# A fused attention and mixture-of-experts kernel: weight tiles moved to the last turns and behind the last stores, late tiles cut into paced pieces

## The chip, the cores and the metric

One core of a Trainium2 chip. The metric is device microseconds of one execution; before the change three runs gave 456.1, 458.65 and 459.66 us, a median of 458.65 us.

## The reference: what is computed

```python
# attention: q, k, v of (8 batches, 8 heads, 576 rows, 64)
scores = 0.125 * q @ k.T ; masked to blocks of 64: block_i >= block_j
attn = exp(scores - max) / (sum + 1e-9) ; x = attn @ v      # x: (4608 tokens, 512)
# experts: 8, capacity 80
expert = argmax(x @ w_gate) ; gate = softmax value of it
for e in range(8):
    tok = the up to 80 tokens of expert e with the highest gate
    out[tok] = gate[tok] * (relu(x[tok] @ w1[e]) @ w2[e])    # w1[e]: 512x1024, w2[e]: 1024x512
# all other rows of out are zero; everything is float32
```

## The kernel before, in words

**Attention.** The work is 32 head pairs (8 batches of 4). A loop of turns `i` runs the list TURN: in turn `i` pair `i` makes its scores and its softmax, pair `i-1` its transposes and values, pair `i+1` is prepared (`prep`: a transpose of q or k on VectorE, for q also a scaling on GpSimd), pair `i+3` is loaded (eight loads of 72 KB in runs of 128 bytes, from SyncE) and the v of pair `i+2`. Three buffers `ld` hold the loads, so that SyncE may run up to three pairs ahead. `max_4` (L459 in the trace) comes once in every turn. After the four pairs of a batch its attention output (unnormalised, in the tile Y) is stored to a DRAM scratch `xs` by four transfers of 288 KB from SyncE (`store`, L289), with the reciprocal row sums beside it (L286, L287), and the gate's logits are made. While this runs, GpSimd writes 18 blocks of 512 KB of zeros to the output.

**Between.** After the last pair come, in a chain on VectorE, TensorE, ScalarE and GpSimd, the last batch's logits and gate, the choice of tokens by expert, and the token numbers `gi`. Then GpSimd issues eight gathers (`xg`, L745) of 80 rows of `xs` each, one for each expert. The first one waits for `gi` and for all stores to `xs`.

**Experts.** For each expert: the rows are normalised and transposed, 128 small matmuls give the hidden layer (`ps`, L845), 128 more the output (`av`, L845), which is transposed back, scaled and scattered. Each matmul has its own weight load. The 16 weight tiles of 2 MB (w1[0], w1[1], w2[0], w1[2], w2[1], ...) have nine buffers: three are there during attention (pool `wp`), six lie where attention's buffers were (`fwa`, `fwc`, `fwb`). The three early tiles are loaded by six transfers of 1 MB from GpSimd in turns 6, 10, 14, 18, 22 and 26 (`early`, L590). All 13 others come from SyncE (`weights`, L242), 2 MB each: six wait for the second gather's data, the other seven for a buffer, that is for the matmuls that read the tile nine places earlier.

**What sets the order.** Attention and the last batch's gate stand in the order of the program (a manual schedule). What follows is placed by a planner with a timeline of its own, queue by queue. Each queue runs its instructions in its order; an instruction that waits holds up those behind it.

Of the kernel before, what the change touches and what calls it, by code (L numbers as in the profile page):

```python
# [18 lines left out]
P = 128  # L19
BLK = 64  # L20
NT = 5
FW0, FWA, FWC, FWB = 3, 3, 1, 2
WARM = [8, 14, 5, 2, 12]
NCAND = 12
CHUNK = 80
# [53 lines left out]
def tile_attn_moe(ctx, tc, q, k, v, w_gate, w1, w2, capacity, out, xs=None, dbg=None):  # L79
    nc = tc.nc  # L80
    B, H, S, D = q.shape
# [20 lines left out]
    if xs is None:  # L102
        xs = dram.tile([NTOK, XW], F32, name="xs")
# [18 lines left out]
    for i in range(4):  # L122
        r = slice(32 * i, 32 * i + 32)
# [19 lines left out]
    rows = 2 * P  # L143
# [25 lines left out]
    before = const.tile([P, P], F32, name="before")  # L169
    after = const.tile([P, P], F32, name="after")  # L170
# [51 lines left out]

    wlist = [(w1, 0)] + [x for e in range(E) for x in ((w1, e + 1), (w2, e))][0:-2] + [(w2, E - 1)]
    wt_ = {}

    def early():
        for w_, view in ((wt_[src is w2, e], src[e].rearrange("(a p) f -> p a f", p=P)) for src, e in wlist[0:FW0]):
            na = w_.shape[1]
            for a in range(0, na, na // 2):
                yield w_[:, a:a + na // 2], view[:, a:a + na // 2]  # L230

    def weights(n, after=None):

        nonlocal nw
        for _ in range(n):
            src, e = wlist[nw]
            w_ = wpools[nw % len(wpools)].tile([P, KP * F], F32, name="w")
            nw += 1
            wt_[src is w2, e] = w_ = w_.rearrange("p (a f) -> p a f", f=src.shape[2])
            if nw <= FW0:  # L240
                continue
            load = nc.sync.dma_start(w_, src[e].rearrange("(a p) f -> p a f", p=P))  # L242
            if after is not None:
                tc.add_manual_dep(load.ins, after.name, mybir.DependencyInfo(
                    mybir.DependencyClass.Sync, mybir.DependencyReason.DATA))

# [14 lines left out]
    class Batch:  # L263
# [17 lines left out]

            nc.vector.transpose(self.Y[:, :, pr], self.xT[:, pr])

        def store(self):
            rows = xs[self.b * S:(self.b + 1) * S]
            nc.sync.dma_start(rows[0:512, DM:DM + H].rearrange("(t p) h -> p t h", p=P), self.rs[:, 0:NT - 1])  # L286
            nc.sync.dma_start(rows[512:S, DM:DM + H], self.rs[0:BLK, NT - 1])  # L287
            for i in range(4):
                self.stored = nc.sync.dma_start(rows[:, i * P:(i + 1) * P].rearrange("(j r) c -> r j c", r=32),  # L289
                                                self.Y[32 * i:32 * i + 32].rearrange("r j a c -> r j (a c)"))  # L290

# [262 lines left out]
    n = B * NP  # L554
    pairs = [Pair(i) for i in range(n)]
# [15 lines left out]
    with tc.manual_schedule():  # L571
        warm(WARM[0], ps_m.tile([P, 512], F32, name="pm"))
        constants()
        constants2()
        for i in range(-3, n + 2):
            if i == -1:
                nc.sync.dma_start(ci, capacity.bitcast(U32).partition_broadcast(P))
                for h in range(2):
                    nc.sync.dma_start(wgd[h * D:(h + 1) * D, :, h * E:(h + 1) * E], wg_v[h])

            if i >= 4 and (i % 2 or i % 8 == 4) and i < n:
                clear(cleared)
                cleared += 1
            if i == 5:
                capacities()
            if i == 4:
                weights(FW0)
                halves = early()
            if i in range(6, 6 + 8 * FW0, 4):
                nc.gpsimd.dma_start(*next(halves))  # L590
            for d, what, *args in TURN:
                if what == "step":
                    step()
                elif 0 <= i + d < n and not (what == "flip" and i + d >= n - NP):
                    getattr(pairs[i + d], what)(*args)
            if n - NP <= i - 1 < n:
                pairs[i - 1].flip()
            if i >= 2 and (i - 2) % NP == NP - 1 and i - 2 < n - 1:
                bt = batches[(i - 2) // NP]
                todo += [(bt.recip,), (bt.store,), (bt.logits, 0), (bt.logits, 1), (bt.logits2, 0), (bt.logits2, 1), (bt.gate,),  # L600
                         (bt.turn, nc.gpsimd)] + [(bt.turn2,)]
        while cleared < nz:
            clear(cleared)
            cleared += 1
        while todo:
            step()
        bt = batches[B - 1]
        bt.recip()
        bt.store()
        bt.logits(0)  # L610
        bt.logits(1)
        bt.logits2(0, (3, NT))
        bt.logits2(1, (3, NT))
        bt.gate()
        bt.turn(nc.vector, 2)
        bt.turn2()
# [16 lines left out]
    tw = dict(reuse_waits="tile")  # L633
    fwa = late.enter_context(tc.tile_pool(name="fwa", bufs=FWA, **right, **tw))
    wpools += [fwa] * FWA
    sel2 = late.enter_context(tc.tile_pool(name="sel2", bufs=1, **right, **tw))


# [41 lines left out]
    HOLD = 1  # L680
# [59 lines left out]
    xg, fetches = [], []  # L740
# [82 lines left out]
    fwc = late.enter_context(tc.tile_pool(name="fwc", bufs=FWC, **right, **tw))  # L823
    fwb = late.enter_context(tc.tile_pool(name="fwb", bufs=FWB, **tw))
    wpools += [fwc] * FWC + [fwb] * FWB
    weights(FWA + FWC + FWB, fetches[HOLD])

    def divide(dst, src):

# [270 lines left out]
```

## Time and profile before

| | |
|---|---|
| runs | 456.1, 458.65, 459.66 us |
| the profiled execution | 455.05 us, its span 453.2 us |
| TensorE busy | 409.2 us (90% of the span) |
| VectorE, ScalarE, GpSimd busy | 283.5, 271.4, 67.7 us |
| mean granted clock of TensorE | 0.975 |
| data moved | 84.41 MB, 64.91 of them on SyncE's hardware queue, 18.16 on GpSimd's software queue |
| packets under 512 bytes | 196925 of 230219 |

How to read it: the profiled execution lies 3.6 us below the median of the three runs and 1.05 us below the fastest of them. Busy shares are means over stages with different limits. The span has three: attention up to about 324 us from its start, the choice of tokens up to about 343 us, the experts up to 445 us. A row of a timeline begins with its start and its length in us; "SPq" and "POOLq" are the queues of SyncE and GpSimd, whose DMA rows show the issuing alone, and the data lands later.

### The profile page before, as it was taken

To read this page: it belongs to the slowest core of one execution; us is meant where nothing else is said; L and a number is where in the kernel's file an instruction comes from. 1 tells how busy PE (TensorE), PEld (TensorE's weight loads), DVE (VectorE), ACT (ScalarE), POOL (GpSimd) and SP (SyncE) were. 2 spreads that over 40 slices of the span, in tenths; PEclk is the share of its full clock that TensorE was granted. 3 is DMA by queue.
4 is the path that set the end of the run, shared out by engine and by line. 5 is a ranking of instruction groups with operands and counts; after the bars stand their busy time and mean duration, and the time that the engine had idled before them with its cause. 6 is when DMAs were issued, how large, how long until landed. Compare 5 with 4: busy or idle time off the path is not lost.

```text
span 453.2 us, 15524 instructions
## 1 busy us (share of the span) xinstructions
PE 409.2 (90%) x6427; PEld 290.4 (64%) x6427; DVE 283.5 (63%) x564; ACT 271.4 (60%) x863; POOL 67.7 (15%) x136
## 2 busy tenths in 40 slices
PE   5899999999999999999999899799868888887991
PEld 3566666666666666666666566465647777777981
DVE  5667887888798798788878679585763212111111
ACT  1688888788798788878878697578321201010100
POOL 5001120111021012111102111010037000000010
PEclk9699999999999999999999999989997999999997
DMA  9678898798889789889779787855047999999110
GB/s 130 103 128 168 172 199 173 140 227 173 186 164 226 133 192 200 194 165 223 163 125 195 174 189 138 174 131 106 15 93 233 352 397 400 394 398 381 45 32 19
DMA packets 230219, 84.41 MB, mean 186 GB/s; under 512 B 196925, under 2 KB 215357, under 8 KB 230144
## 3 DMA queue, kind: packets, MB, share of 16 engines
q1 hardware_dynamic: 222528, 64.91, 64.0%
q0 software_dynamic: 5248, 18.16, 11.8%
q8 instruction: 52, 0.85, 0.8%
q10 hardware_dynamic: 2368, 0.30, 0.5%
q14 instruction: 23, 0.19, 0.1%
HBM read 63.21 MB, written 20.33 MB: 184 GB/s over the span
## 4 chain that ended last, share of the span: by engine, by line
PE 73%; DVE 7%; DMA 6%; SPq 4%; issue 4%; ACT 4%; POOL 0%; POOLq 0%; ACTq 0%; DVEq 0%
PE pm L529 19%; PE sc L434 13%; PE pm L499 9%; PE ps L845 9%; PE av L845 8%; PE sc L450 7%; DMA ld<-in_q_dram 4%; SPq L401 2%; DVE negm L459 2%; PE pm L299 2%; ACT P L468 2%; SPq L289 2%; PE pm L482 1%; ACT P L463 1%; DVE negm L455 1%
## 5 line engine op out<-in xcount | busy, mean ns | idle before, releaser
L463 ACT ACTIVATE P<-sc,negm 128x128 f32<-128x128 f32 (+3 forms) x256 | 133.1, 530 | 23.2 <-DVE negm L455 21.4
L455 DVE TENSOR_REDUCE negm<-sc 128x2 f32<-128x1024 f32 (+3 forms) x128 | 100.1, 809 | 36.6 <-PE sc L441 36.5
L434 PE MATMUL sc<-T,T 64*128 64x128 f32 (+3 forms) x512 | 94.1, 466 | 9.0 <-ACT P L463 7.5
L499 PEld LDWEIGHTS pm<-ident,P 64*128 64x128 f32 x1536 | 57.2, 141 | 33.5 <-ACT P L468 10.0
L499 PE MATMUL pm<-ident,P 64*128 64x64 f32 x1536 | 69.6, 231 | 1.9 <-DVE prod L317 0.4
L434 PEld LDWEIGHTS sc<-T,T 64*128 64x128 f32 x512 | 42.1, 189 | 30.0 <-ACT P L463 10.7
L529 PE MATMUL pm<-PT,vn 128*64 128x128 f32 (+1 forms) x512 | 60.7, 379 | 0.0
L419 POOL TENSOR_SCALAR T<-T 128x576 f32<-128x576 f32 x32 | 21.3, 665 | 235.0 <-DVE T L416 191.2
L416 DVE STREAM_TRANSPOSE T<-ld 128x576 f32<-128x576 f32 x64 | 48.7, 761 | 10.2 <-DMA ld<-in_q_dram 10.1
L463 ACT ACTIVATION_READ_ACCUMULATOR P<-sc,negm 128x1 f32 x256 | 52.8, 206 | 0.0
L529 PE MATMUL pm<-PF,vn 128*64 128x64 f32 (+1 forms) x768 | 48.6, 249 | 0.9 <-ACT PF L539 0.9
L529 PEld LDWEIGHTS pm<-PT,vn 128*64 128x64 f32 x512 | 33.5, 137 | 22.9 <-issue 22.9
L845 PE MATMUL ps<-xsT,w 128*64 128x80 f32 x1024 | 40.7, 239 | 6.8 <-issue 6.8
L539 ACT COPY PF<-pm 128x512 f32<-128x512 f32 x64 | 34.4, 589 | 16.4 <-PE pm L499 16.4
L541 DVE COPY PT<-pm 128x512 f32<-128x512 f32 x64 | 43.5, 680 | 0.5 <-PE pm L499 0.5
L845 PEld LDWEIGHTS ps<-xsT,w 128*64 128x64 f32 x1024 | 38.3, 141 | 8.5 <-issue 8.0
L845 PE MATMUL av<-hT,w 128*64 128x80 f32 x1024 | 38.4, 234 | 5.5 <-issue 5.5
L845 PEld LDWEIGHTS av<-hT,w 128*64 128x64 f32 x1024 | 36.5, 137 | 7.5 <-issue 7.5
L450 PE MATMUL sc<-T,T 64*64 64x288 f32 x256 | 39.4, 427 | 0.6 <-ACT P L463 0.6
L539 ACT COPY PT<-pm 128x512 f32<-128x512 f32 x64 | 37.8, 590 | 0.0
L865 ACT ACTIVATE hT<-ps 128x320 f32<-128x320 f32 x16 | 7.0, 437 | 51.1 <-PE ps L845 51.1
L529 PEld LDWEIGHTS pm<-PF,vn 128*64 128x64 f32 x768 | 32.3, 138 | 7.5 <-ACT PF L539 1.1
(166 smaller groups left out, 390.1 us busy)
## 6 DMA issues: line engine op xcount, KB each, us to landing
w<-in_moe_w_dram SPq DMA_DIRECT2D x13, 2048.0 KB, 21.3
ld<-in_q_dram SPq DMA_DIRECT2D x128, 72.0 KB, 3.5
out_dram<-zero POOLq DMA_DIRECT2D x18, 512.0 KB, 4.0
xs<-Y SPq DMA_DIRECT2D x32, 288.0 KB, 5.0
ld<-in_k_dram SPq DMA_DIRECT2D x124, 72.0 KB, 2.9
vn<-in_v_dram SPq DMA_DIRECT2D x64, 128.0 KB, 3.2
w<-in_moe_w_dram POOLq DMA_DIRECT2D x6, 1024.0 KB, 6.5
vt<-in_v_dram SPq DMA_DIRECT2D x32, 32.0 KB, 3.0
```

What stands on the lines that cost most here:

```text
L289: self.stored = nc.sync.dma_start(rows[:, i * P:(i + 1) * P].rearrange("(j r) c -> r j c", r=32), self.Y[32 * i:32 * i + 32].rearrange("r ...
L416: nc.vector.transpose(t, self.nat[x].rearrange("p g d -> p (g d)"))
L419: nc.gpsimd.tensor_scalar(t, t, scalar1=SCALE, scalar2=1.0, op0=ALU.mult, op1=ALU.mult)
L434: nc.tensor.matmul(s[:, h, c:c + P * (u + 1)], lhsT=self.T[0][r, P * u:P * (u + 1)], rhs=self.T[1][r, 0:P * (u + 1)], start=(x == 0), stop ...
L450: nc.tensor.matmul(s[r, c, 0:288], lhsT=self.T[0][r, 512:S], rhs=self.T[1][r, 288 * c:288 * (c + 1)], start=True, stop=True)
L455: nc.vector.tensor_reduce(self.negm[:, u], self.s[g][:, :, c:c + P * (u + 1)], axis=AX.X, op=ALU.max, negate=True)
L463: nc.scalar.activation(Pt[self.i % 2][u][:, h], self.s[g][:, h, c:c + P * (u + 1)], AF.Exp, bias=self.negm[:, u, h:h + 1], scale=1.0, accu ...
L499: nc.tensor.transpose(pt[c][:, n_ * BLK:(n_ + 1) * BLK], from_[r, P * j:P * (j + 1)], ident[r, r])
L529: nc.tensor.matmul(to, lhsT=lhs, rhs=rhs, start=(n_ == 0), stop=(n_ == len(steps) - 1))
L539: nc.scalar.copy(*self.out.pop((what, x)))
L541: nc.vector.tensor_copy(*self.out.pop((what, x)))
L845: yield nc.tensor.matmul(dst(b)[64 * c:64 * (c + 1)], lhsT=w_[:, a, col:col + 64], rhs=x_[:, a], start=(a == 0), stop=(a == n - 1))
```

## The change

- Four tiles are early (FW0 4 instead of 3; FWB 1 instead of 2, so still nine buffers). Each is one transfer of 2 MB from GpSimd, one in each of the turns 28 to 31, in place of the six of 1 MB in turns 6 to 26.
- The last batch's x is stored pair by pair (`store_pair`): four transfers of 72 KB in runs of 128 bytes for each pair, 16 in all, in place of four transfers of 288 KB in runs of 512 bytes after the last pair.
- Two more tiles (w2[1], w1[3]) are asked for right after attention's buffers are closed, without a wait for a gather, as whole transfers of 2 MB.
- The other ten tiles are loaded in four pieces of 512 KB each. A piece waits for the landing of the third piece before it. The first three of these tiles still wait for the second gather, the other seven for a buffer.

```diff
--- before.py
+++ after.py
@@ -19,7 +19,8 @@
 P = 128
 BLK = 64
 NT = 5
-FW0, FWA, FWC, FWB = 3, 3, 1, 2
+FW0, FWA, FWC, FWB = 4, 3, 1, 1
+PARTS, UNDERWAY = 4, 3
 WARM = [8, 14, 5, 2, 12]
 NCAND = 12
 CHUNK = 80
@@ -222,14 +223,9 @@
 
     wlist = [(w1, 0)] + [x for e in range(E) for x in ((w1, e + 1), (w2, e))][0:-2] + [(w2, E - 1)]
     wt_ = {}
-
-    def early():
-        for w_, view in ((wt_[src is w2, e], src[e].rearrange("(a p) f -> p a f", p=P)) for src, e in wlist[0:FW0]):
-            na = w_.shape[1]
-            for a in range(0, na, na // 2):
-                yield w_[:, a:a + na // 2], view[:, a:a + na // 2]
-
-    def weights(n, after=None):
+    parts_ = []
+
+    def weights(n, after=None, parts=PARTS):
 
         nonlocal nw
         for _ in range(n):
@@ -238,11 +234,16 @@
             nw += 1
             wt_[src is w2, e] = w_ = w_.rearrange("p (a f) -> p a f", f=src.shape[2])
             if nw <= FW0:
+                nc.gpsimd.dma_start(w_, src[e].rearrange("(a p) f -> p a f", p=P))
                 continue
-            load = nc.sync.dma_start(w_, src[e].rearrange("(a p) f -> p a f", p=P))
-            if after is not None:
-                tc.add_manual_dep(load.ins, after.name, mybir.DependencyInfo(
-                    mybir.DependencyClass.Sync, mybir.DependencyReason.DATA))
+            view = src[e].rearrange("(a p) f -> p a f", p=P)
+            na = w_.shape[1]
+            for a in range(0, na, na // parts):
+                load = nc.sync.dma_start(w_[:, a:a + na // parts], view[:, a:a + na // parts]).ins
+                for before in ((after,) if after is not None else ()) + tuple(parts_[-UNDERWAY:][:1] if len(parts_) >= UNDERWAY else ()):
+                    tc.add_manual_dep(load, before.name, mybir.DependencyInfo(
+                        mybir.DependencyClass.Sync, mybir.DependencyReason.DATA))
+                parts_.append(load)
 
 
 
@@ -281,11 +282,17 @@
 
             nc.vector.transpose(self.Y[:, :, pr], self.xT[:, pr])
 
-        def store(self):
+        def store_pair(self, pr):
+            rows = xs[self.b * S:(self.b + 1) * S]
+            for i in range(4):
+                nc.sync.dma_start(rows[:, i * P + 32 * pr:i * P + 32 * pr + 32].rearrange("(j r) c -> r j c", r=32),
+                                  self.Y[32 * i:32 * i + 32, :, pr])
+
+        def store(self, whole=True):
             rows = xs[self.b * S:(self.b + 1) * S]
             nc.sync.dma_start(rows[0:512, DM:DM + H].rearrange("(t p) h -> p t h", p=P), self.rs[:, 0:NT - 1])
             nc.sync.dma_start(rows[512:S, DM:DM + H], self.rs[0:BLK, NT - 1])
-            for i in range(4):
+            for i in range(4 if whole else 0):
                 self.stored = nc.sync.dma_start(rows[:, i * P:(i + 1) * P].rearrange("(j r) c -> r j c", r=32),
                                                 self.Y[32 * i:32 * i + 32].rearrange("r j a c -> r j (a c)"))
 
@@ -583,11 +590,8 @@
                 cleared += 1
             if i == 5:
                 capacities()
-            if i == 4:
-                weights(FW0)
-                halves = early()
-            if i in range(6, 6 + 8 * FW0, 4):
-                nc.gpsimd.dma_start(*next(halves))
+            if n - 4 <= i < n - 4 + FW0:
+                weights(1)
             for d, what, *args in TURN:
                 if what == "step":
                     step()
@@ -595,6 +599,7 @@
                     getattr(pairs[i + d], what)(*args)
             if n - NP <= i - 1 < n:
                 pairs[i - 1].flip()
+                pairs[i - 1].bt.store_pair(pairs[i - 1].pr)
             if i >= 2 and (i - 2) % NP == NP - 1 and i - 2 < n - 1:
                 bt = batches[(i - 2) // NP]
                 todo += [(bt.recip,), (bt.store,), (bt.logits, 0), (bt.logits, 1), (bt.logits2, 0), (bt.logits2, 1), (bt.gate,),
@@ -606,7 +611,7 @@
             step()
         bt = batches[B - 1]
         bt.recip()
-        bt.store()
+        bt.store(False)
         bt.logits(0)
         bt.logits(1)
         bt.logits2(0, (3, NT))
@@ -633,6 +638,7 @@
     tw = dict(reuse_waits="tile")
     fwa = late.enter_context(tc.tile_pool(name="fwa", bufs=FWA, **right, **tw))
     wpools += [fwa] * FWA
+    weights(2, parts=1)
     sel2 = late.enter_context(tc.tile_pool(name="sel2", bufs=1, **right, **tw))
 
 
@@ -823,7 +829,7 @@
     fwc = late.enter_context(tc.tile_pool(name="fwc", bufs=FWC, **right, **tw))
     fwb = late.enter_context(tc.tile_pool(name="fwb", bufs=FWB, **tw))
     wpools += [fwc] * FWC + [fwb] * FWB
-    weights(FWA + FWC + FWB, fetches[HOLD])
+    weights(FWA - 2 + FWC + FWB, fetches[HOLD])
 
     def divide(dst, src):
 
```

Where the instructions now stand. First SyncE's queue at the end of attention (`ld`, `vn` and `vt` are loads of q, k and v, `xs<-Y` stores of x, `xs<-rs` of the row sums, `w` weight tiles). Before:

```order
L409 DMA vn<-in_v_dram 128x4x64 x2
L411 DMA vt_136<-in_v_dram 64x2x64
L286 DMA xs<-rs 128x4x8
L287 DMA xs<-rs 64x8
L289 DMA xs<-Y 32x18x128 x4
L286 DMA xs<-rs 128x4x8
L287 DMA xs<-rs 64x8
L289 DMA xs<-Y 32x18x128 x4
L242 DMA w<-in_moe_w_dram 128x4x1024
L242 DMA w<-in_moe_w_dram 128x8x512
```

Of the change:

```order
L418 DMA vt_136<-in_v_dram 64x2x64
L288 DMA xs<-Y 32x18x32 x4
L293 DMA xs<-rs 128x4x8
L294 DMA xs<-rs 64x8
L296 DMA xs<-Y 32x18x128 x4
L288 DMA xs<-Y 32x18x32 x8
L242 DMA w<-in_moe_w_dram 128x8x512
L242 DMA w<-in_moe_w_dram 128x4x1024
L288 DMA xs<-Y 32x18x32 x4
L293 DMA xs<-rs 128x4x8
L294 DMA xs<-rs 64x8
L242 DMA w<-in_moe_w_dram 128x2x512 x4
```

Before, the stores of the last two batches stood ahead of all weights. Now two tiles of 2 MB stand behind the third pair's stores and ahead of the last pair's four stores and the row sums.

Second, GpSimd's queue in the last turns (`T` is the scaling of q, once in a turn; `zero` the clearing of the output). Before:

```order
L419 TENSOR_SCALAR T_4236<-T_4236 128x576
L590 DMA w<-in_moe_w_dram 128x4x512
L419 TENSOR_SCALAR T_4384<-T_4384 128x576
L150 DMA out_dram<-zero 128x1024
L419 TENSOR_SCALAR T_4549<-T_4549 128x576
L150 DMA out_dram<-zero 128x1024
L270 MEMSET sums 64x8
L419 TENSOR_SCALAR T_4720<-T_4720 128x576
L356 TENSOR_TENSOR sp<-Gm,sameE 128x320
L150 DMA out_dram<-zero 128x1024
L419 TENSOR_SCALAR T_4884<-T_4884 128x576
L419 TENSOR_SCALAR T_5022<-T_5022 128x576
```

Of the change:

```order
L151 DMA out_dram<-zero 128x1024
L237 DMA w<-in_moe_w_dram 128x4x1024
L271 MEMSET sums 64x8
L426 TENSOR_SCALAR T_4713<-T_4713 128x576
L363 TENSOR_TENSOR sp<-Gm,sameE 128x320
L151 DMA out_dram<-zero 128x1024
L237 DMA w<-in_moe_w_dram 128x4x1024
L426 TENSOR_SCALAR T_4879<-T_4879 128x576
L237 DMA w<-in_moe_w_dram 128x8x512
L426 TENSOR_SCALAR T_5023<-T_5023 128x576
L151 DMA out_dram<-zero 128x1024
L237 DMA w<-in_moe_w_dram 128x4x1024
```

The scalings in the first list are those of pairs 26 to 31, in the second those of pairs 29 to 31. The last 1 MB stood between the scalings of pairs 26 and 27; now 2 MB stand ahead of the scaling of pair 29, 2 MB ahead of that of pair 30, 2 MB ahead of that of pair 31, and 2 MB behind it.

## Rows read from the trace of the kernel before

**Rows 1.** Page: busy us by engine; DMA share by slices; queue of instructions.

```profile
PE 409.2 (90%) x6427; PEld 290.4 (64%) x6427; DVE 283.5 (63%) x564; ACT 271.4 (60%) x863; POOL 67.7 (15%) x136
...
DMA  9678898798889789889779787855047999999110
...
q8 instruction: 52, 0.85, 0.8%
```

**Rows 2.** Timeline of VectorE, L459: start, length; one in each turn.

```profile
205.76 0.72 DVE L459 TENSOR_REDUCE negm<-sc 128x1 f32<-128x576 f32 x1
...
233.82 0.76 DVE L459 TENSOR_REDUCE negm<-sc 128x1 f32<-128x576 f32 x1 [0.41 <-PE sc L450]
243.64 0.72 DVE L459 TENSOR_REDUCE negm<-sc 128x1 f32<-128x576 f32 x1
...
284.13 0.72 DVE L459 TENSOR_REDUCE negm<-sc 128x1 f32<-128x576 f32 x1
297.93 0.76 DVE L459 TENSOR_REDUCE negm<-sc 128x1 f32<-128x576 f32 x1 [1.40 <-PE sc L450]
...
317.00 0.76 DVE L459 TENSOR_REDUCE negm<-sc 128x1 f32<-128x576 f32 x1 [1.09 <-PE sc L450]
```

**Rows 3.** Chain of waits, 200 to 290 us: start, length, what.

```profile
285.87 3.76 DMA ld<-in_q_dram
```

**Rows 4.** Timeline of SyncE's queue: start and length of the issuing.

```profile
78.07 4.23 SPq L401 DMA_DIRECT2D ld<-in_q_dram  x4
...
111.87 0.54 SPq L286 DMA_DIRECT2D xs<-rs  x1
...
232.94 0.54 SPq L286 DMA_DIRECT2D xs<-rs  x1
...
238.17 4.40 SPq L401 DMA_DIRECT2D ld<-in_q_dram  x4
```

**Rows 5.** Timeline of VectorE: transposes of q of pairs 10 and 26.

```profile
93.47 0.76 DVE L416 STREAM_TRANSPOSE T<-ld 128x576 f32<-128x576 f32 x1
...
246.11 0.78 DVE L416 STREAM_TRANSPOSE T<-ld 128x576 f32<-128x576 f32 x1 [1.02 <-DMA ld<-in_q_dram]
```

**Rows 6.** Groups by line, TensorE, 344 to 445 us: busy, mean ns, idle before.

```profile
L845 PE MATMUL ps<-xsT,w 128*64 128x80 f32 x1024 | 40.7, 239 | 6.8 <-issue 6.8
L845 PE MATMUL av<-hT,w 128*64 128x80 f32 x1024 | 38.4, 234 | 5.5 <-issue 5.5
```

**Rows 7.** Timeline of TensorE: the first and the last of the idle pieces.

```profile
355.54 2.02 PE L845 MATMUL ps<-xsT,w 128*64 128x80 f32 x52 [0.98 <-issue]
...
418.50 3.95 PE L845 MATMUL ps<-xsT,w 128*64 128x80 f32 x107 [1.38 <-issue]
```

**Rows 8.** Stretches: length, busy time by engine, clock, DMA share, GB/s.

```profile
354.00:418.00 64.00, 52.17 (x1292) 48.39 (x1287) 9.81 (x30) 6.67 (x16) 3.75 (x4) 1.00 1.04 392
418.00:444.00 26.00, 24.31 (x635) 23.18 (x635) 3.71 (x6) 1.75 (x4) 2.74 (x3) 1.00 0.15 49
```

**Rows 9.** Timeline of GpSimd: two clearings of the output, start and length.

```profile
267.19 0.58 POOL L150 DMA_DIRECT2D out_dram<-zero  x1
...
282.43 0.59 POOL L150 DMA_DIRECT2D out_dram<-zero  x1
```

**Rows 10.** Timeline of VectorE: Y of pair 30 is ready after this.

```profile
319.50 0.77 DVE L282 STREAM_TRANSPOSE Y<-xT 128x576 f32<-128x576 f32 x1
```

**Rows 11.** Chain of waits, 290 to 453 us: the first gather's issue begins.

```profile
338.17 0.03 POOLq L745
```

**Rows 12.** DMA view, 317 to 340 us, in 40 slices of 0.575 us.

```profile
GB/s 0 0 0 0 28 0 0 0 0 0 0 0 0 0 0 0 18 13 45 177 177 179 173 175 181 282 198 181 182 117 16 0 0 0 0 0 0 0 0 0
```

**Rows 13.** Page, DMA issues: count, KB each, median us to landing.

```profile
w<-in_moe_w_dram SPq DMA_DIRECT2D x13, 2048.0 KB, 21.3
...
xs<-rs SPq DMA_DIRECT2D x8, 2.0 KB, 1.7
```

**Rows 14.** Timeline of SyncE's queue: the first late weight tiles.

```profile
343.90 6.87 SPq L242 DMA_DIRECT2D w<-in_moe_w_dram  x3
```

## The prediction, made before the changed kernel ran

> **What bounds the kernel now.** I read the page's slices first, then the chain of waits, the timelines of VectorE and SyncE through attention, and the stretches of the expert stage. TensorE is busy for most of the span, so what counts is where it stands still. There are two such places, and the DMA engines are behind both [rows 1].
>
> Attention first. L459 comes once in a turn, so it is a clock. From 205.76 to 243.64 us a batch of four turns takes 37.88 us [rows 2]; this is TensorE's own pace. From 243.64 to 317.00 there are seven turns in 73.36 us; at the pace before they would take 37.88 + 28.06 (205.76 to 233.82) = 65.94. So 7.4 us are lost at the end of attention, most in one turn (284.13 to 297.93, 13.8 us), and there the chain goes through a load of q [rows 3]. The reason is a slow drift. SyncE issues without a break, and its stores of the row sums come every (232.94 - 111.87)/3 = 40.4 us [rows 4], 2.5 us slower than the batches. The lead melts: q of pair 10 was all issued at 82.3 and used at 93.5, a lead of 11.2 us; q of pair 26 at 242.6 and 246.1, a lead of 3.5 us, and that is where VectorE first waits for data [rows 4, 5]. Under about 3.5 us there is a stall.
>
> Experts next. L845 is busy for 79 us and has 12.3 us of idle time, put down to nothing that the profile shows [rows 6]. It is in eleven pieces of about 1.1 us, one every 6.3 us, from 355 to 418 us [rows 7]. From 354 to 418 the DMA engines are full (share 1.04, 392 GB/s) and TensorE is idle for 11.8 us of 64; from 418 on, at a share of 0.15, the pieces are gone [rows 8]. The weights are never waited for. One piece comes for each 128 matmuls with their 128 weight loads, and TensorE's instructions come by DMA in 52 packets of 16 KB for 12854 instructions, about 247 each [rows 1]. I read the pieces as blocks of instructions that arrive late while the DMA engines are full. So this stage is bound by TensorE, and fewer bytes help only by making the full stretch shorter or its queue shallower.
>
> **The change, part by part.**
>
> *Six early loads leave turns 6 to 26.* That is 1 MB a batch, at 392 GB/s [rows 8] 2.7 us of all DMA engines. 40.4 - 2.7 = 37.7 us a batch, just under the batch's 37.9: the drift stops and the lead stays near 11 us. The 7.4 us of stall go. Bounds: 0 (the drift has another cause) and 7.4.
>
> *Four loads of 2 MB come in turns 28 to 31.* The first two stand on GpSimd's queue just behind the clearings at 267 and 282 us [rows 9], the others later. Each takes 2.1 MB/392 GB/s = 5.35 us. The first delays the loads of pair 30, the second those of pair 31; no q or k comes later. 11.2 - 5.35 = 5.9 us of lead is enough for pair 30; 11.2 - 10.7 = 0.5 us is 3 us too little for pair 31 if nothing is caught up between. I take 1 us, bounds 0 and 3. The issuing itself (0.6 us for 512 KB [rows 9], so at most 2.4) costs nothing: GpSimd is busy for 15% of the span [rows 1], and without that cover q's scaling would be late by it.
>
> *Pair stores and two tiles ahead of the last of them.* The two tiles wait on SyncE for pair 30's stores, which wait for Y at 319.50 + 0.77 = 320.3 [rows 10]. Behind SyncE's tiles stand pair 31's stores and the row sums, and for these the first gather waits, now issued at 338.17 [rows 11]. Price of one pair's stores (295 KB in runs of 128 bytes, not in the trace): 1.7 us at the 178 GB/s of the present stores [rows 12], 4.2 us as the equally shaped q loads of a pair take under load [rows 4]; 3 us, between. Two tiles: 4.2 MB/392 = 10.7 us. Issue 0.5, stores 3, tiles 10.7, stores 3, landing 1.7 (as for the row sums [rows 13]): 320.3 + 18.9 = 339.2. The gather starts 1 us late; bounds 0 (all done at 336.6) and 3.8 (at 341.6, with 4.2 twice). Today's stores end at about 334 [rows 12], so this cover of 4 us is spent. An earlier end of attention moves both alike.
>
> *Ten tiles after the second gather instead of thirteen.* From 343.9 [rows 14], ten times 5.35 us end at 397.4 instead of about 418. The pieces of idle time between 397 and 418 go: three of eleven, 3.4 us. The buffers don't hold this up: tile 9 waits for the first block of matmuls, and each next one for a block that is done before the transfer's turn.
>
> *Pieces of 512 KB, three under way.* Now SyncE keeps several 2 MB transfers queued (21.3 us to landing [rows 13]); then there are at most 1.6 MB, 4 us at 392 GB/s. Whether a block of instructions gets through sooner is not in the trace. From below 0 (fewer queued bytes give no reason for a loss), from above the whole 8 x 1.12 = 9.0 us of the remaining pieces; I take half, 4.5 us, because they are late by 1.1 us only and the queue ahead becomes several times shorter while the engines stay as full. The Trainium skill, page "DMA: Bandwidth & Descriptors", section "Bandwidth", speaks against this: it says to batch transfers to 1 MiB or more, and gives 2.0 us plus bytes over 436 GB/s for each. By it a single 512 KB piece takes an estimated 3.2 us, 164 GB/s, if one had to end before the next.
>
> **Sum.** -7.4 + 1.0 + 1.0 - 3.4 - 4.5 = -13.3 us, on the profiled execution's 455.05 us: 441.7. That execution lies 3.6 us below the median of 458.65. Part of this spread may be the stalls that go, so I add half of it: **443.5 us**.
>
> **The rivals.** All on the same footing (455.05 + 1.8).
>
> *The idle pieces vanish.* If a block of instructions waits only for the piece in transfer, 512 KB or 1.3 us, it isn't late any more: -7.4 + 1 + 1 - 12.3 = -17.7, 439. The Trainium skill, page "DMA: Bandwidth & Descriptors", section "Queues, rings and completion order", says that an engine goes round its queues and changes only between packets, which would bear this out if a packet is bounded by the transfer. For it: the delay seen is small. Against: the engines stay full. 0.17.
>
> *The pieces stay, the gather is late.* Only three go, and the stores take their upper price: -7.4 + 1 + 3.8 - 3.4 = -6.0, 451. 0.14.
>
> *The gain of attention is spent.* The drift goes on in part (zeros and stores have a share in it), 6 us of stall remain, the gather is 3.8 late, the pieces stay: -7.4 + 6 + 3.8 - 3.4 = -1.0, 456. 0.09.
>
> *Slower: the big early loads starve the last pairs.* If the 1 MB loads are not what eats the lead, pair 26 still has 3.5 us, and 10.7 us of new loads fall on pairs 30 and 31 with no lead left. Stall in the last turns 7.4 + 10.7 instead of 7.4, gather +1, idle pieces -3.4: +8.3, 465. It decides from a lead of under about 4 us at pair 30 ahead of the first 2 MB. For it: two loads of double size close together; against: 40.4 - 2.7 = 37.7. 0.04.
>
> *Slower: the pacing starves TensorE.* The last block of 128 matmuls takes 79.1/16 = 4.9 us [rows 6] and ends at about 444 [rows 8], so the last tile is used from about 439 now, 431 with the other gains. Ten tiles from 343.9 must then move at 241 GB/s, 1.6 MB in 6.5 us. A piece takes 1.7 us (the landing of a tiny transfer [rows 13]) plus 1.3 us of transfer, so three under way need 3 to 4 us. Only if each had to land before the next, 40 pieces of 3 us, would the last tile land at 464, 33 us late, and the end be 476. The Trainium skill's rule on batching, taken alone, leads here. 0.02.
>
> *It doesn't do what it says* has no room: the order of both queues shows the moved transfers.
>
> **How the numbers follow.** The forecast has 0.54. For this kernel 1% is 4.6 us, about what a measurement can tell from none: faster means under 454. Forecast and the first two rivals give 0.85 for faster, the third 0.09 for the same, the last two 0.06 for slower. The range holds the forecast with its bounds and the first two rivals: 436 (all pieces gone, no stall, no late gather, 455.05 - 19.7 = 435.4) to 453 (the second rival and 2 us of stall); 0.15 of the other cases stay out.
>
> **What would show it.** L459 has even turns up to the last batch, and SyncE's row sums come every 37.9 us or have gaps of waiting between. The lead at pair 26 is 10 us or more. The first gather is issued within 4 us of `gi`, and if late, it is held by DMA `xs<-Y` or `xs<-rs`. The idle pieces before L845 sum to 3 to 8 us instead of 12.3 and end 54 us after the second gather. It would be wrong if L459 still has a turn of over 11 us without a batch's end, if the pieces number eleven again, or if L845 waits for a DMA `w`.

## The result and the profile after

| | before | changed |
|---|---|---|
| runs of the comparison | 456.1 to 461.91 us, median 459.15 | 451.04 to 453.07 us, median 451.56 |
| ratio | | 0.9883, 95% interval 0.9841 to 0.9926 |
| the profiled execution, its span | 455.05, 453.2 us | 451.06, 448.9 us |

The change gains 7.6 us of 459, where 15 were forecast against the median (13.3 on the profiled execution, which shows 4.0). The gains that were forecast came, 19.3 us by the balance below; three new losses took 16.3 of them back. An idle piece is, as in the prediction, a stretch in which TensorE stands still between expert matmuls and nothing that the profile shows holds it.

VectorE's timeline, `max_4` (L466 now, one in each turn; beside [rows 2]):

```profile
204.34 0.72 DVE L466 TENSOR_REDUCE negm<-sc 128x1 f32<-128x576 f32 x1
...
242.22 0.72 DVE L466 TENSOR_REDUCE negm<-sc 128x1 f32<-128x576 f32 x1
...
280.11 0.72 DVE L466 TENSOR_REDUCE negm<-sc 128x1 f32<-128x576 f32 x1
289.09 0.76 DVE L466 TENSOR_REDUCE negm<-sc 128x1 f32<-128x576 f32 x1 [0.41 <-PE sc L457]
307.81 0.76 DVE L466 TENSOR_REDUCE negm<-sc 128x1 f32<-128x576 f32 x1 [2.03 <-PE sc L457]
317.86 0.76 DVE L466 TENSOR_REDUCE negm<-sc 128x1 f32<-128x576 f32 x1 [1.09 <-PE sc L457]
```

Both batches up to 280.11 take 37.88 and 37.89 us: TensorE's own pace, now to the end of the seventh batch. Then one turn takes 18.72 us. From the second to the third pair of a batch it is 9.0 us elsewhere, so this turn lost 9.7 us. VectorE's wait in it, and SyncE's queue (start and length of issuing):

```profile
299.38 0.78 DVE L423 STREAM_TRANSPOSE T<-ld 128x576 f32<-128x576 f32 x1 [8.24 <-DMA ld<-in_q_dram]
```

```profile
224.77 5.47 SPq L408 DMA_DIRECT2D ld<-in_q_dram  x4
...
251.26 2.07 SPq L408 DMA_DIRECT2D ld<-in_k_dram  x4
...
262.85 10.63 SPq L408 DMA_DIRECT2D ld<-in_q_dram  x4
273.58 5.19 SPq L408 DMA_DIRECT2D ld<-in_k_dram  x4
281.02 12.35 SPq L408 DMA_DIRECT2D ld<-in_q_dram  x4
...
324.39 1.14 SPq L242 DMA_DIRECT2D w<-in_moe_w_dram  x2
325.65 12.32 SPq L288 DMA_DIRECT2D xs<-Y  x4
338.07 1.38 SPq L293 DMA_DIRECT2D xs<-rs  x1
```

The first row is q of pair 26: all issued at 230.2, used at 243.57, a lead of 13.3 us where it was 3.5 [rows 4, 5]. The drift is gone. The rows of 10.63 and 12.35 us are q of pairs 30 and 31. In experiment 5, where no early tile stands beside them, the same loads are issued in 5.9 and 3.2 us; the row of 2.07 us, of k, has four loads of this shape at about their fastest. What stands beside them here is in GpSimd's timeline:

```profile
263.63 0.77 POOL L237 DMA_DIRECT2D w<-in_moe_w_dram  x1
...
278.40 0.59 POOL L151 DMA_DIRECT2D out_dram<-zero  x1
278.99 0.78 POOL L237 DMA_DIRECT2D w<-in_moe_w_dram  x1
283.00 0.96 POOL L237 DMA_DIRECT2D w<-in_moe_w_dram  x1
```

The early tiles are numbered in the order of their issuing. Tile 1 falls on pair 30. On pair 31 fall a clearing, tile 2 **and tile 3**: 4.7 MB.

The chain of waits at the gather (beside [rows 11]):

```profile
339.00 0.18 DVE gi L741
339.19 0.26 SPq L293
...
339.49 2.30 DMA xs<-rs
341.80 0.03 POOLq L751
```

`gi` is ready at 339.18, the gather's issue begins at 341.80; it waits 2.6 us for row sums that stood on SyncE behind the two tiles.

The groups of TensorE from 344 to 445 us (busy, mean ns, idle before; beside [rows 6]) and two stretches (beside [rows 8]):

```profile
L851 PE MATMUL ps<-xsT,w 128*64 128x80 f32 x1024 | 42.2, 243 | 3.6 <-issue 3.6
L851 PE MATMUL av<-hT,w 128*64 128x80 f32 x1024 | 37.7, 234 | 0.1
```

```profile
364.00:400.00 36.00, 35.02 (x899) 33.30 (x899) 7.41 (x25) 4.51 (x11) 2.83 (x3) 1.00 0.90 309
400.00:424.00 24.00, 22.99 (x596) 21.81 (x594) 2.97 (x5) 2.60 (x6) 1.83 (x2) 1.00 0.85 290
```

Of 12.3 us of idle pieces 3.6 are left. The DMA engines aren't full any more (share 0.90 instead of 1.04) and nothing waits for a weight. But the first block of 128 expert matmuls is longer. Before, on TensorE's timeline:

```profile
345.23 6.12 PE L845 MATMUL ps<-xsT,w 128*64 128x80 f32 x128
```

Now:

```profile
348.96 2.72 PE L851 MATMUL ps<-xsT,w 128*64 128x80 f32 x39
352.01 0.23 PE L851 MATMUL ps<-xsT,w 128*64 128x80 f32 x1 [0.33 <-issue]
352.73 0.27 PE L851 MATMUL ps<-xsT,w 128*64 128x80 f32 x1 [0.49 <-issue]
353.44 0.27 PE L851 MATMUL ps<-xsT,w 128*64 128x80 f32 x1 [0.45 <-issue]
354.15 4.88 PE L851 MATMUL ps<-xsT,w 128*64 128x80 f32 x86 [0.44 <-issue]
```

It takes 10.0 us instead of 6.1, with 1.7 us of the remaining idle pieces in it.

**The balance of the two spans.** Attention begins 1.5 us earlier (first `max_4` pair 16.68 and 25.70, before 16.57 and 27.16; the change does nothing there, and this first turn takes between 9.0 and 10.6 us in the other runs, so it is chance). The end of attention -7.4 + 9.7. From the last `max_4` to `gi` +0.2. Gather +2.6, from its issue to the first matmul +0.1. First block +4.0. From its end to the last `av` matmul 91.6 before, 79.7 now: -11.9 (10.4 of it idle pieces). Sum -4.2 us; with 0.1 after the last matmul, the difference of the spans.

### The profile page after: what moved, and what is told of

Same layout as the page of the kernel before. It is cut to its first block, busy times and chain, and to the rows that moved or that the text cites. A ratio compares the mean times of both kernels' runs of the same rounds, so it can differ in the third digit from the quotient of the medians.

```text
span 448.9 us, 15577 instructions
## 1 busy us (share of the span) xinstructions
PE 409.9 (91%) x6427; PEld 291.8 (65%) x6427; DVE 283.7 (63%) x564; ACT 271.7 (61%) x863; POOL 66.1 (15%) x134
## 4 chain that ended last, share of the span: by engine, by line
PE 74%; DMA 7%; DVE 7%; SPq 5%; ACT 4%; issue 2%; POOL 0%; POOLq 0%; ACTq 0%; DVEq 0%
PE pm L536 19%; PE sc L441 13%; PE pm L506 9%; PE ps L851 9%; PE av L851 8%; PE sc L457 7%; DMA ld<-in_q_dram 5%; SPq L408 3%; DVE negm L466 2%; ACT P L475 2%; PE pm L306 2%; PE pm L489 1%; PE pm L885 1%; ACT P L470 1%; DVE negm L462 1%
## 5 line engine op out<-in xcount | busy, mean ns | idle before, releaser
L506 PEld LDWEIGHTS pm<-ident,P 64*128 64x128 f32 x1536 | 56.8, 140 | 33.5 <-ACT P L475 10.6
L851 PE MATMUL ps<-xsT,w 128*64 128x80 f32 x1024 | 42.2, 243 | 3.6 <-issue 3.6
L851 PEld LDWEIGHTS ps<-xsT,w 128*64 128x64 f32 x1024 | 39.7, 145 | 5.4 <-issue 4.8
L475 ACT ACTIVATE P<-sc,negm 128x576 f32<-128x576 f32 x32 | 23.7, 740 | 23.5 <-DVE negm L466 23.5
L851 PE MATMUL av<-hT,w 128*64 128x80 f32 x1024 | 37.7, 234 | 0.1
L546 ACT COPY PT<-pm 128x512 f32<-128x512 f32 x64 | 37.7, 590 | 0.0
## 6 DMA issues: line engine op xcount, KB each, us to landing
w<-in_moe_w_dram POOLq DMA_DIRECT2D x4, 2048.0 KB, 12.6
```

Source lines behind the costliest of these rows:

```text
L475: nc.scalar.activation(Pt[self.i % 2][4][:, 0:S].rearrange("p (c k) -> p c k", c=2), self.s["4"][:, :, 0:288], AF.Exp, bias=self.negm[:, 4 ...
L506: nc.tensor.transpose(pt[c][:, n_ * BLK:(n_ + 1) * BLK], from_[r, P * j:P * (j + 1)], ident[r, r])
L546: nc.scalar.copy(*self.out.pop((what, x)))
L851: yield nc.tensor.matmul(dst(b)[64 * c:64 * (c + 1)], lhsT=w_[:, a, col:col + 64], rhs=x_[:, a], start=(a == 0), stop=(a == n - 1))
```

## The experiments

The first four ran on one chip beside 19 runs of the kernel before (median 452.54 us), the next four on another beside 19 (454.17), then three beside 7 (455.87) and one beside 13 (455.51). Ratios are to these; they need not be the quotients of the medians. "The change" below is the changed kernel. How late a gather is, is counted from `gi` to the row of its issuing on GpSimd: 0.9 us in the kernel before, 3.7 in the change.

**1. Early tiles two turns later.**

```diff
-            if n - 4 <= i < n - 4 + FW0:
+            if n - 2 <= i < n - 2 + FW0:
```

Expected: 

> The change with the four early tiles two turns later, in turns 30 to 33, so that they come behind the q and k loads of pair 31. Theory (the second, third and a clearing fall on the loads of pair 31, and SyncE can't issue until they are through): the one stalled turn of 18.7 us goes back to 9.0, minus 9.7 us, 442 us; at most 3 us of it are given back where the first gather waits for stores that stand behind the later tiles. Rival (the stall comes from the stores of the batch before and the clearing, or from the drift): the turn stays above 15 us, 450 to 452 us.

Measured: 445.52 us, ratio 0.9799 [0.9727, 0.9871]. No turn above 10.1 us is left at the end of attention and `gi` is ready at 332.0, 7 us earlier than in the change. The stall is due to the early loads. But the first gather is issued only at 341.4, 9.4 us after `gi`. SyncE's queue:

```profile
312.45 6.38 SPq L288 DMA_DIRECT2D xs<-Y  x8
318.93 6.69 SPq L242 DMA_DIRECT2D w<-in_moe_w_dram  x2
325.71 10.82 SPq L288 DMA_DIRECT2D xs<-Y  x4
336.62 1.38 SPq L293 DMA_DIRECT2D xs<-rs  x1
```

The last pair's stores, 295 KB, take 10.8 us to issue behind 4.2 MB of tiles. The gather is 9.4 us late instead of 3.7, so more than half of the stall's 9.7 us is lost again; expected were at most 3.

**2. The two tiles behind the last stores.**

```diff
-            nc.sync.dma_start(rows[512:S, DM:DM + H], self.rs[0:BLK, NT - 1])
+            self.stored = nc.sync.dma_start(rows[512:S, DM:DM + H], self.rs[0:BLK, NT - 1])
...
-    weights(2, parts=1)
+    with tc.issue_after(batches[B - 1].stored.ins):
+        weights(2, parts=1)
```

Expected: 

> The change with the two tiles of 2 MB behind the last pair's stores and row sums on SyncE's queue, early tiles as in the change. Theory (the gather is 2.6 us late because the stores stand behind 4.2 MB, and the longer wait lets TensorE's clock fall, so that the first block of 128 matmuls takes 10.0 instead of 6.0 us): the first gather is issued within 0.5 us of gi and the first block takes 6 to 7 us, minus 6 us, 445 us. Rival 1 (the stores are slow in themselves, in runs of 128 bytes): the gather stays 2 us late or more, 449 to 452 us. Rival 2 (the two tiles now run under the gathers): issue in time, landing 3 us later, 448 to 451 us.

Measured: 447.43 us, ratio 0.9852 [0.9777, 0.9926]; profiled 445.78 against the change's 451.06. The long turn stays (19.1 us), and the gather is issued 0.9 us after `gi`: SyncE's order made it late. It lands in 4.5 us, where the first gather of the change takes 3.1, so the second rival has a small part. The first block takes 7.0 us and has no idle piece:

```profile
347.29 7.03 PE L852 MATMUL ps<-xsT,w 128*64 128x80 f32 x128
```

This is the length of the theory, though not by its reason: the mean granted clock of this block is 0.64, no higher than the 0.71 of the change's.

**3. All ten late tiles whole, no pacing.**

```diff
-PARTS, UNDERWAY = 4, 3
+PARTS, UNDERWAY = 1, 99
```

Expected: 

> The change with its ten late tiles as whole transfers of 2 MB, unpaced, all else as in the change. Theory (pieces and pacing let the blocks of instructions through): idle time before the expert matmuls goes from 3.6 us back to about 8 pieces of 1.1 us, plus 6 to 8 us, 458 us. Rival (three tiles fewer are enough): idle stays under 5 us, 451 to 453 us.

Measured: 457.55 us, ratio 1.0101 [1.0059, 1.0143]. The groups, and the same stretch as above:

```profile
L851 PE MATMUL ps<-xsT,w 128*64 128x80 f32 x1024 | 41.5, 242 | 5.5 <-issue 5.5
L851 PE MATMUL av<-hT,w 128*64 128x80 f32 x1024 | 38.2, 234 | 4.5 <-issue 4.5
```

```profile
364.00:400.00 36.00, 29.31 (x744) 27.38 (x742) 6.80 (x22) 3.26 (x8) 1.93 (x2) 1.00 1.04 395
```

The DMA engines move 395 GB/s instead of 309, and TensorE runs 744 matmuls instead of 899. Three tiles fewer take away 2.3 us of idle pieces, pieces and pacing together the rest; these two were not tried apart.

**4. Pieces and pacing alone,** in the kernel before (its 13 late tiles in four pieces, three under way; nothing else).

```diff
...
-            load = nc.sync.dma_start(w_, src[e].rearrange("(a p) f -> p a f", p=P))
...
+            for a in range(0, na, na // parts):
+                load = nc.sync.dma_start(w_[:, a:a + na // parts], view[:, a:a + na // parts]).ins
...
```

Expected: 

> The kernel before with its thirteen late tiles in pieces of 512 KB, three under way, nothing else. Theory (pieces and pacing do it): idle before the expert matmuls falls from 12.3 to 2 to 4 us, 449 us against 459. Rival (the fewer tiles do it): idle 9 us or more, 456 to 459 us. If the pacing slows the weights themselves, the expert matmuls wait for a DMA w, and the time is above 459.

Measured: 453.56 us, ratio 1.001 [0.9966, 1.0055]; the profiled execution took 456.86 us, more than all but one of this run's ten. The groups:

```profile
L852 PE MATMUL ps<-xsT,w 128*64 128x80 f32 x1024 | 42.3, 244 | 7.0 <-DMA w<-in_moe_w_dram 6.6 <-issue 0.3
L852 PE MATMUL av<-hT,w 128*64 128x80 f32 x1024 | 38.7, 234 | 3.2 <-DMA w<-in_moe_w_dram 2.2 <-SPq L920 0.7
```

The idle pieces are gone, but TensorE now waits 8.8 us for weights in this execution, and the theory's 449 us don't come. At the paced rate (322 GB/s from 364 to 400) 13 tiles come too late; ten don't. The six early loads stand in turns 6 to 26 here, and the stall at the end of attention is there as in the kernel before (a turn of 13.9 us).

**5. Experiments 1 and 2 together.**

Expected: 

> Both mends at once: early tiles in turns 30 to 33 and the two tiles behind the last pairs' stores. Theory (the stall is two 2 MB loads and a clearing on pair 31's loads; the gather is late because stores stand behind the tiles): no max_4 spacing over 11 us, gi's end near 332 us, first gather issued within 2 us of it, against 9.4 us with later tiles alone; profiled time near 438, median 437 to 441. Rival (the stores are slow of themselves under the early loads that now lie next to them, whatever stands ahead of them): gather still 6 to 9 us late, 444 to 446. Rival 2 (the late tiles only land later instead, and the expert matmuls wait for weights): gather in time, but idle time before the expert matmuls grows by 3 to 6 us to 6 to 8 us, 442 to 445.

Measured: 440.51 us, ratio 0.9714 [0.9647, 0.978], the fastest of its group. `gi` is at 331.2 and the gather's issue at 332.1, with no long turn. The median is in the theory's range, the profiled 439.98 us 2 us over its 438, for the gather takes longer to land. From the chain of waits:

```profile
332.08 7.11 DMA xg<-xs,gi
```

In the change this step takes 3.0 us (there it is the second gather; the first takes 3.1). The two tiles now lie on the gather instead of on the stores.

**6. Early tiles in turns 28, 31, 32, 33.**

```diff
-            if n - 4 <= i < n - 4 + FW0:
+            if i in (n - 4, n - 1, n, n + 1):
```

Expected: 

> Early tiles in turns 28, 31, 32, 33 instead of 28 to 31: of the loads, only number 1 keeps its place. Theory (numbers 2 and 3 with a clearing between them fell on pair 31's loads): no max_4 spacing over 11 us, last max_4 some 7 to 9 us earlier than in the change; the gather stays late behind the tiles, by some 9 us as with later tiles alone, so 443 to 447. Rival (number 1 on pair 30's loads uses up the lead and is the start of the stall): a spacing of 13 us or more remains, at pair 30 or 31, time 448 to 452.

Measured: 447.63 us, ratio 0.9867 [0.9807, 0.9927]. No long turn (288.98 to 297.99 us); the last `max_4` is 9.8 us earlier than in the change; the gather is issued 10.7 us after `gi`. Tile 1 alone makes no stall, but it isn't harmless: it pushes pair 31's loads back. SyncE's rows of q of pairs 30 and 31, first with tile 1 (this run), then without an early tile beside them (experiment 5):

```profile
262.48 8.90 SPq L408 DMA_DIRECT2D ld<-in_q_dram  x4
...
279.56 2.86 SPq L408 DMA_DIRECT2D ld<-in_q_dram  x4
```

```profile
264.48 5.93 SPq L408 DMA_DIRECT2D ld<-in_q_dram  x4
...
274.83 3.16 SPq L408 DMA_DIRECT2D ld<-in_q_dram  x4
```

The turns of experiment 5 run 1.8 us later (`max_4` at 281.81 against 280.00), so against them pair 31's q begins 6.5 us later with tile 1. In the change, by the same count, it is 7.9 us. By these rows this q would have been issued before tile 2 left, had tile 1 not been there.

**7. Five more warming matmuls** ahead of the experts.

```diff
-WARM = [8, 14, 5, 2, 12]
+WARM = [8, 14, 5, 2, 17]
```

Expected: 

> The change with five more warming matmuls before the expert matmuls and nothing else. Theory (the first block of 128 expert matmuls took 10.0 us instead of 6.1 because the granted clock was at its lower level longer): the block 6 to 7 us, clock over 0.85 in it, time 3 us under the change's. Rival (its pieces of idle time and the loads beside it make it long): the block stays at 9 to 10 us and the time within 1 us of the change's.

**8. The change once more.**

Expected: 

> The change itself, unaltered, beside the three others. Both theories: within 1.5 us of the time that it had at first against the same kernel before (ratio 0.984 to 0.993), one spacing of max_4 near 19 us, first block of expert matmuls 9 to 11 us if the lower clock there belongs to the change and 6 to 8 if it was an accident of that execution.

Measured: 452.23 us, ratio 0.9959 [0.9931, 0.9987], with more warming; 452.54, ratio 0.9967 [0.9929, 1.0004], without. The first block of the repeated change, then of the one with more warming:

```profile
348.52 2.96 PE L851 MATMUL ps<-xsT,w 128*64 128x80 f32 x40
352.50 0.26 PE L851 MATMUL ps<-xsT,w 128*64 128x80 f32 x1 [1.03 <-issue]
353.21 0.23 PE L851 MATMUL ps<-xsT,w 128*64 128x80 f32 x1 [0.44 <-issue]
353.91 3.24 PE L851 MATMUL ps<-xsT,w 128*64 128x80 f32 x86 [0.48 <-issue]
```

```profile
350.07 3.20 PE L851 MATMUL ps<-xsT,w 128*64 128x80 f32 x43
353.81 0.38 PE L851 MATMUL ps<-xsT,w 128*64 128x80 f32 x3 [0.54 <-issue]
355.24 3.06 PE L851 MATMUL ps<-xsT,w 128*64 128x80 f32 x82 [1.05 <-issue]
```

The block takes 8.6 and 8.2 us, with 1.95 and 1.6 us of idle pieces near matmul 40 in both, as in the first execution (1.7). So about 2 us of the +4.0 come back in every execution and are idle pieces. The 1.4 us that the first execution has more lie behind them: the last 86 matmuls take 4.88 us there at a mean granted clock of 0.65, and 3.24 us in the repeat at 1.00 (0.50 is the lower level, 1.2 GHz; 1.00 the upper, 2.4 GHz). With more warming it is 1.00 too, but in experiments 6 and 10 the stretch behind the pieces has 0.64 and 0.65, so it isn't an accident of one execution. The first 40 or so matmuls run at or near the lower level in all of them: 0.50 in the kernel before, 0.57 in the change's first execution, 0.51 in the repeat and with more warming. The clock theory falls in this form: the longer wait for the gather didn't make the block's start slower, and more warming bought nothing. The ratio of the change itself is nearer to 1 here than at first (0.9967 against 0.9883) and outside the 0.984 to 0.993 expected: its gain is small. Whether the chip makes this difference is not shown.

**9 to 11. Variants of the fastest version.** The two tiles behind the stores in pieces with three under way; one tile there and eleven paced ones later; and the last batch's x stored whole again.

```diff
-        weights(2, parts=1)
...
+        weights(2)                  # 9; in 10: weights(1, parts=1), and FWA - 1 later on
```

```diff
-                pairs[i - 1].bt.store_pair(pairs[i - 1].pr)      # 11
...
-        bt.store(False)
+        bt.store()
```

Expected, 9: 

> The version with later early tiles and with the two tiles behind the last stores, but these two tiles now also in 512 KB pieces with three under way. With whole tiles the first gather took 7.1 us to land under them, against 3.0 in the change. Theory (what slows the gather is the number of bytes queued beside it): landing 3.5 to 5.5 us, the first expert matmul 2 to 3 us earlier, time 2 to 3 us under the version with whole tiles (440.5), so 437.5 to 438.5. Rival (it is the full DMA engines, whatever the size of the queue): landing still 6.5 to 8 us and the same time, 440 to 441.

Expected, 10: 

> The version with later early tiles and the tiles behind the last stores, with one tile there instead of two and eleven paced ones behind the second gather. Theory (the tiles ahead delay the gather by the bytes that are still queued, but eleven paced tiles at 295 to 320 GB/s can't all be in time): the first gather lands in 3.5 to 5 us instead of 7.1, but 2 to 4 us of waiting for weights come in the expert matmuls; time 439 to 442, no better than 440.5. Rival (two tiles ahead are not needed): no wait for weights, 437 to 438.

Expected, 11: 

> The version with later early tiles and the tiles behind the last stores, with the last batch of x stored whole after its last pair again instead of pair by pair. Theory (storing by pairs gains only what the last store ends earlier; the store of a batch takes 6.6 us in the kernel before and has 13 us until the first gather): first gather still within 2 us of gi's end and the time within 1.5 us of the 440.5 with pair stores. Rival (the whole store now collides with the early loads beside it and is not done in time): gather 4 to 8 us late, time 444 to 448.

Measured, in this order: 439.15, 440.91 and 440.39 us; ratios 0.9628 [0.9563, 0.9692], 0.9696 [0.9631, 0.9762], 0.9677 [0.9611, 0.9743]. The gather lands in 5.4, 5.8 and 6.4 us instead of 7.1 (in 11 the chain shows the second one; VectorE uses the first 6.6 us after its issuing). In 9 the first matmul still begins at 342.71, as in 5, since the second expert's rows, transposed ahead of it, are normalised only at 341.1; in 10 it begins 3.0 us earlier, and the first block gives 1.9 back (8.8 us with two idle pieces instead of 6.9). No weight is waited for in 10, against its theory; its rival's 437 us didn't come either. Storing whole costs nothing here, so the stores by pairs bring nothing in this version. The three don't differ beyond their intervals, nor from 5.

**12. Early tiles in turns 28, 29, 32, 33:** only tile 3 leaves pair 31's loads (and tile 4 goes later).

```diff
-            if n - 4 <= i < n - 4 + FW0:
+            if i in (n - 4, n - 3, n, n + 1):
```

Expected: 

> Early tiles in turns 28, 29, 32, 33 instead of 28 to 31: number 2 keeps its place just behind a clearing and ahead of pair 31's loads, number 3 goes. Theory (numbers 2, 3 and the clearing, 4.7 MB, all go ahead of or between pair 31's loads, and each adds its own time at some 375 GB/s): without number 3's 2.1 MB the loads of pair 31 land some 5.6 us earlier, VectorE waits for them 2 to 4 us instead of 8.2, and the long turn is 12 to 14 us instead of 18.7. Rival (number 2 alone is enough, the loads suffer alike from any 2 MB beside them): the turn stays at 16 us or more. Rival 2 (the forecast's price, 0 to 3 us, holds for number 2 and only number 3 was missed): no turn over 11 us. The gather is late behind the tiles in all three, so the time says little: 444 to 450.

Measured: 453.02 us, ratio 0.9941 [0.9903, 0.998], over the 444 to 450 expected; the gather is 15.0 us late here. What was asked is in VectorE's timeline:

```profile
290.33 0.76 DVE L466 TENSOR_REDUCE negm<-sc 128x1 f32<-128x576 f32 x1 [0.41 <-PE sc L457]
293.49 0.78 DVE L423 STREAM_TRANSPOSE T<-ld 128x576 f32<-128x576 f32 x1 [1.12 <-DMA ld<-in_q_dram]
...
300.17 0.76 DVE L466 TENSOR_REDUCE negm<-sc 128x1 f32<-128x576 f32 x1 [0.89 <-PE sc L457]
```

Pair 31's q is waited for 1.1 us instead of 8.2, and the turn takes 9.8 us instead of 18.7. From the start of its issuing to its use it takes 11.9 us (281.62 to 293.49) instead of 18.4 (281.02 to 299.38): tile 3's 2.1 MB were worth 6.5 us, 5.6 were expected. The wait is under the theory's 2 to 4 us and the turn under 11: the second rival holds. With tiles 1 and 2 in place, it is tile 3 that makes the long turn; no run has tiles 2 and 3 without tile 1.

## Why the prediction was wrong

**The step that failed** is "Four loads of 2 MB come in turns 28 to 31", taken at 1 us with bounds 0 and 3: it cost 9.7. "The first delays the loads of pair 30, the second those of pair 31; no q or k comes later" left the third out. The order of GpSimd's queue showed it ahead of pair 31's scaling, and nothing on GpSimd waits between the scaling of pair 30 and this issue, so it left at 283.0, two us after pair 31's first load. The price per load was about right: where 5.35 us were forecast, tile 3 held pair 31's q up by 6.5 us (12), and tile 1 pushed it back by 6.5 to 7.9 (6). Nor was it wrong to add up the first two on pair 31: without tile 3 VectorE waits 1.1 us for it (12), near the 1 us taken. With the third added at the forecast's own 5.35 us, its "3 us too little" becomes 8.4; 9.7 were lost. Not shown is how the DMA engines share out between the two queues; the runs show only that 2.1 MB more on the other queue moved the use of pair 31's q by 6.5 us.

**Attention's drift**: right. -7.4 us, even turns until 280, a lead of 13.3 us. Row sums now come every (256.84 - 144.86)/3 = 37.3 us (40.4 before), 37.7 forecast. All runs without the six early loads have even turns up to the last batch, and experiment 4, which keeps them, has the old stall.

**Pair stores and two tiles**: 2.6 us for 1.0, inside the bounds of 0 to 3.8, by the mechanism named; experiment 2 takes it away. (By the prediction's own sum the upper one is 341.6 - 338.2 = 3.4.) What failed here is "An earlier end of attention moves both alike": in experiment 1 `gi` is 7.2 us earlier than in the change, the row of the gather's issuing only 1.4, and in experiments 1, 6 and 12 it comes 9 to 15 us after `gi`. The stores have early tiles beside them there too, but these alone don't make the gather late: in experiment 5, with the same early tiles and without the two tiles ahead, the row sums are all issued by 327.5, 3.8 us before `gi`.

**Idle pieces**: 8.7 us gone, 7.9 forecast. The split was off: whole tiles keep ten of the 12.3 us (3), so fewer tiles give 2.3 and not 3.4, and pieces some 6.4 and not 4.5. The rows have four pieces after 397.4 where the forecast took three; experiment 3 has nine of the eleven left. That blocks of instructions come late behind queued data fits all four kernels: 12.3, 10.0 and 3.6 us in the kernel before, experiment 3 and the change, and 0.3 in experiment 4; that the instruction queue itself is held up was not measured apart. Two readings support it. The packets of the instruction queue (q8 of the DMA view) go with TensorE's instructions: 10 for 2579 of them from 354 to 418 us of the kernel before, 5 for 1270 from 418 to 444, about 255 each. And the pieces keep their lengths: the third to the ninth of experiment 3 (1.64, 0.92, 1.15, 1.02, 1.16, 0.95 and 1.09 us) are, in order and within 0.01 us, those of the kernel before, 5 us later, so they belong to places in the row of instructions. The Trainium skill, page "DMA: Bandwidth & Descriptors", section "Bandwidth", asks for transfers of 1 MiB or more. The traces agree on the rate (395 GB/s whole, 309 in pieces); the time goes the other way here, for pieces win. The formula that the prediction takes from this page of the Trainium skill stands in its section "Anatomy of one DMA", for transfers that GpSimd issues; the pieces here come from SyncE, and three under way land in a median of 5.0 us.

**Not in the sum**: the first block of expert matmuls, +4.0: about 2 us of idle pieces, which recur, and in the first execution a lower clock behind them. What brings pieces there stays open. Full DMA engines alone don't: their share in the first block is 1.03 in the change and 1.00 and 1.01 in experiments 2 and 5, which have no piece there and take 7.0 and 6.9 us.

**The range.** 451.56 us lies within 436 to 453, and beside the 451 of the second rival. Both are luck: that rival keeps all but three of the pieces and has no long turn, and the number came from a stall, a late gather and a first block that took back gains larger than forecast. The prediction's own sign of being wrong, a turn of over 11 us without a batch's end, came.

Of the rivals none came as described. "The big early loads starve the last pairs" had the place, though not its reason, a lead that stays low: the lead was there, and three tiles and a clearing used it up. Pacing makes TensorE wait for weights only with 13 tiles left (4).

## What to carry to other kernels

When a load moves to another queue, list every transfer that this queue can issue without waiting until the next consumer's data has landed, not one for each turn; a queue with nothing to wait for runs ahead. Count too what each transfer pushes back on the other queue: a load that causes no wait by itself can put the next one beside those that do. Put bulk loads behind the small stores and loads that something waits for, on every queue: taking a load off one short transfer here put it on the next (stores, then the gather). Where an engine stands still while the DMA engines are full and waits for no data, fewer bytes under way can be worth more than rate, as long as the paced rate still meets the last use.

## What the runs showed of the hardware

- Four loads of 72 KB in runs of 128 bytes, issued in 5.9 us (pair 30, behind stores) and 3.2 us (pair 31) with no early tile beside them (experiment 5), took 10.6 and 12.4 us to issue while 2 MB transfers ran on GpSimd's queue; those 2 MB took a median of 12.6 us to land where 2.1 MB at the 392 GB/s of [rows 8] are 5.4.
- Four stores of the same shape behind 4.2 MB of tiles took 10.8 to 12.3 us to issue; the first four of the last batch, with no late tile ahead, 2.8 to 3.5 us (experiments 1, 5 and 6).
- Behind idle pieces near matmul 40 of the first block the granted clock was 0.65 in the change and in experiment 10, 1.00 in the change's repeat.
- Pieces of 512 KB with three under way land in a median of 5.0 us and move 290 to 322 GB/s; whole 2 MB tiles move 392 to 395.
